# Two spectral mixings and two attentions on one core: first rows scaled and paired by TensorE, checks placed in the attention, the triangle added by TensorE in the last units, last rows folded by tile

## The chip, the core and the metric

The kernel runs on one core of a Trainium2 chip. The time is that of the device in microseconds, the median of several runs; the change is timed against the kernel before on the same chip. The engines are named as in the profile: PE (TensorE, matrix products; PEld are its weight loads), DVE (VectorE), ACT (ScalarE), POOL (GpSimd), SP (the engine that issues most transfers). A profile of one execution shows every instruction with its start and length and what it waited for.

## The reference

A sequence of 2048 rows of 512 numbers passes through four layers, each added to its input: `x = x + A(layernorm(x))`, then `x = x + B(layernorm(x))`, and both once more.

A is a Fourier mixing: the real part of a DFT over the sequence of a DFT over the hidden dimension, `y = Cr @ (x @ Wr) - Ci @ (x @ Wi)` with cosine and sine matrices that are inputs of the kernel.

B is an attention with 32 heads of 16 numbers over four segments of 512 rows. In a segment: causal softmax attention (`mask` adds -1e9 where the key is later than the query), and a read of a memory from the segments before it, `o = g * (phi(q) M) / (phi(q) z) + (1 - g) * softmax(q k^T / 4) v`. After each segment M and z grow by that segment's keys and values. Then `o @ wo`.

All is computed in float32 or in split forms that keep its precision.

## The kernel before, in words

**Folding.** The cosine and sine matrices are symmetric, so rows s, 1024 - s, 1024 + s and 2048 - s of the normalised input can be added and subtracted first, and the sequence DFT is made over an eighth of the rows. `place_folded` does this for a layer A. The rows lie in four groups A, B, C, D of two octants each, in two halves k = 0, 1; `quad(w, k)` is a tile of 128 partitions x 2 x 512. `normalise` computes mean and variance of each row (BATCH_NORM_STATS2, L376), the inverse root (a power on POOL, L381, and a Newton step on DVE), and scales in place (ACT L391, or DVE L389). `half` (L394) makes A-C (D01), A+C (S01), B-D (D32), B+D (S32); `fold_odd` (L400 to L406) mixes D01 and D32 into the tiles `re` and `im`; `fold_even` (L411 to L425) mixes S01 and S32. `contract(ps)` then makes the sequence DFT for one half ps of the output rows: steps `odd` and `even` for the kinds 0 (real) and 1 (imaginary) and the halves k. `odd` has 8 products of 256 columns (`u<-cf,hAB`), `even` 8 of 128 columns (`u<-cf,hS`) and some with a single row or a single column (`u<-rows`, `u<-cmid`). `drain` (L538 to L573) folds the sums back, `hidden(j)` makes the DFT over the hidden dimension and adds the input.

**Checks.** The folding is right only if the matrices given have the symmetry of a DFT. `place_checks` loads them in 68 units of 512 KB (`chk<-in_chk`, issued by SP, L686) and ACT compares each with one number per row (Abs with bias and running sum, L690, and a read of the sum). `verdict` adds all up and gives one bit; if it fails, a plain version follows. 34 units belong to each layer A: the first 20 from slot 6 to 24 of the layer, the others from slot 38 to 56, which is the start of the attention.

**Attention.** `place_attention` cuts a layer B into 32 units, (segment s, group of 8 heads g, half u of the group: 4 heads). For each: `stack` loads queries and keys (`stkq<-scrq`, `stkk<-scrk`, SP L858), which `proj` has stored as three bfloat16 parts; `natural_max` makes the scores row by row (`nat`) and takes each row's maximum on DVE (L887); `max_rows` turns the maxima (`mT`) and sends them into the query stack (`stkq<-mt`); `softmax_values` makes the scores again, transposed, with the maximum subtracted (`sT`), clamps the blocks on the diagonal (ACT Relu, L952), takes the exponential (ACT, L953, `pT`), zeroes the triangle above the diagonal (POOL select, L956), and multiplies by the values (`pv_bank`); `output` divides. `values`, `mem_read`, `mem_update`, `outproj` make the rest. In the last segment of attention 1, `finish` hands each output tile to `take`, which adds it straight into group D of the second fold (L352).

**Order.** Every function is a generator; `place(order, gen, slots)` says in which slots of a written timetable its steps are issued. Attention has 10 slots per unit. a1, b1, a2, b2 are the slots at which the four layers begin (b = a + 56, a2 = b1 + 340). This gives the program order. Products and transposes on PE keep it (`in_order`). On the other engines a planner orders by program order and priority, with its own estimate of when operands are there; `tc.high_priority(offset)` moves instructions ahead, `tc.issue_after(x)` puts an instruction behind x on the same engine. A tile's `tag` names a set of buffers: "wd" has 8, for probabilities `pT`, attention outputs `onat`, fold tiles and checks; "w" has 16, for the attention's weights; "bank" is 7 banks of PSUM and "pv" the eighth.

## Time and profile before

| | us |
|---|---|
| median of 3 runs | 1279.83 (1279.19 to 1283.01) |
| profiled execution | 1287.08 |
| its span, first to last instruction | 1284.9 |
| first product on PE | 23.67 |
| layer A 1 up to the first probabilities | 0 to 174 |
| attention 1 | 174 to 641 |
| layer A 2 and the attention's filling | 641 to 805 |
| attention 2 and the end | 805 to 1285 |

The profile divides the span into 40 slices of 32 us and gives for each engine the busy tenths. Windows give the busy us of each engine in a stretch, with the count of instructions, then the granted clock of PE (1.00 is full), the mean busy share of the 16 transfer engines and GB/s. A line of the timeline has start, length, engine, source line, operation, what is written `<-` what is read, shapes, how many instructions were merged, and in brackets how long the engine was idle before it and what ended that. Nearly all PE instructions carry L85, the helper that keeps their order, so they are told apart by the tiles.

### The profile page before, as it was taken

To read this page: it belongs to the slowest core of one execution; us is meant where nothing else is said; L and a number is where in the kernel's file an instruction comes from. 1 tells how busy PE (TensorE), PEld (TensorE's weight loads), DVE (VectorE), ACT (ScalarE), POOL (GpSimd) and SP (SyncE) were. 2 spreads that over 40 slices of the span, in tenths; PEclk is the share of its full clock that TensorE was granted. 3 is DMA by queue.
4 is the path that set the end of the run, shared out by engine and by line. 5 is a ranking of instruction groups with operands and counts; after the bars stand their busy time and mean duration, and the time that the engine had idled before them with its cause. 6 is when DMAs were issued, how large, how long until landed. Compare 5 with 4: busy or idle time off the path is not lost. (4 is left out here: it accounts for less than half of the span.)

```text
span 1284.9 us, 24191 instructions
## 1 busy us (share of the span) xinstructions
PE 1145.6 (89%) x7462; PEld 740.9 (58%) x7462; DVE 966.6 (75%) x3519; ACT 872.6 (68%) x1980; POOL 462.0 (36%) x826
## 2 busy tenths in 40 slices
PE   1999578999999999988779996989999999999987
PEld 1886344666566666554358864546665666666544
DVE  8777678778877777788485676867788777777872
ACT  2654677877677777777624546858876786778773
POOL 1021333534444444443300122524434443445431
PEclk9899889999999999999878998979998999999998
DMA  7787853433443344352426888524344334433411
GB/s 279 232 317 258 282 175 108 149 116 116 133 134 117 112 130 134 113 182 82 136 81 211 308 278 252 154 85 143 100 149 131 118 100 148 133 100 109 140 52 53
DMA packets 111094, 197.65 MB, mean 154 GB/s; under 512 B 13885, under 2 KB 63043, under 8 KB 110954
## 3 DMA queue, kind: packets, MB, share of 16 engines
q1 hardware_dynamic: 107690, 195.22, 47.6%
q8 instruction: 61, 1.00, 0.3%
q10 hardware_dynamic: 3264, 0.79, 0.3%
q14 instruction: 79, 0.65, 0.2%
HBM read 128.04 MB, written 67.14 MB: 152 GB/s over the span
## 5 line engine op out<-in xcount | busy, mean ns | idle before, releaser
L887 DVE CUSTOM_DVE_ANT_0 junk<-nat,mask 128x512 bf16<-128x512 f32 (+3 forms) x1024 | 500.6, 489 | 140.3 <-PE nat L85 107.4
L953 ACT ACTIVATE pT<-sT 128x512 f32<-128x512 f32 x640 | 370.6, 597 | 24.6 <-PE pv_bank L85 6.8
L956 POOL TENSOR_SCALAR_AFFINE_SELECT pT<-pT 128x256 f32<-128x256 f32 (+1 forms) x448 | 193.8, 446 | 469.9 <-ACT pT L953 429.9
L85 PE MATMUL nat<-stkk,stkq 96*128 96x512 bf16 (+3 forms) x1024 | 241.5, 307 | 46.6 <-DMA stkk<-scrk 19.6
L85 PE MATMUL sT<-stkq,stkk 99*128 99x256 bf16 (+3 forms) x1024 | 251.7, 311 | 20.7 <-DMA stkq<-mt 11.1
L952 ACT ACTIVATE sT<-sT 128x256 f32<-128x256 f32 (+1 forms) x640 | 208.8, 334 | 66.0 <-PE sT L85 58.2
L85 PEld LDWEIGHTS <-stkk 99*128 99x128 bf16 x1024 | 84.0, 100 | 149.4 <-issue 118.9
L85 PE MATMUL pv_bank<-pT,vt 128*17 128x512 f32 (+3 forms) x2048 | 157.0, 445 | 1.8 <-POOL pT L956 1.8
L85 PEld LDWEIGHTS <-stkq 96*128 96x128 bf16 x1024 | 94.3, 100 | 95.2 <-issue 59.9
L85 PE MATMUL pqk<-xT,wq 128*128 128x512 f32 x384 | 127.9, 446 | 4.6 <-ACT xT L97 2.6
L85 PE MATMUL po<-wo,oh 128*128 128x512 f32 x384 | 124.7, 444 | 3.8 <-DVE oh L99 3.0
L85 PE MATMUL pqk<-xT,wk 128*128 128x512 f32 x384 | 126.6, 442 | 0.0
L85 PE MATMUL pvv<-wv,xT 128*128 128x512 f32 x384 | 122.0, 432 | 2.8 <-DVE mx L887 2.8
L690 ACT ACTIVATE chk<-chk,reps 128x1024 f32<-128x1024 f32 (+1 forms) x80 | 81.3, 1017 | 60.4 <-DMA chk<-in_chk 60.1
L85 PEld LDWEIGHTS pv_bank<-pT,vt 128*17 128x17 f32 x2048 | 54.4, 99 | 87.8 <-issue 80.7
L85 PE MATMUL u<-cf,hAB 128*128 128x256 f32 x256 | 68.5, 429 | 34.2 <-DVE hAB L400 23.7
L1024 ACT ACTIVATE ot<-pv_bank 128x512 f32<-128x512 f32 x64 | 38.3, 598 | 70.6 <-PE pv_bank L85 70.6
L887 DVE DVE_READ_ACCUMULATOR2_ANT mx<- 128x1 f32 x1024 | 84.4, 82 | 0.2
L85 PEld LDWEIGHTS po<-wo,oh 128*128 128x128 f32 x384 | 70.3, 197 | 22.8 <-DVE oh L99 5.8
L827 POOL TENSOR_TENSOR parts<-rem,parts 128x512 bf16<-128x512 f32 x60 | 71.9, 1198 | 28.7 <-ACT parts L823 28.3
L85 PEld LDWEIGHTS u<-cf,hAB 128*128 128x128 f32 x256 | 54.7, 218 | 44.3 <-DVE hAB L400 23.7
L85 PEld LDWEIGHTS pqk<-xT,wq 128*128 128x128 f32 x384 | 70.2, 194 | 16.9 <-ACT xT L97 3.0
(200 smaller groups left out, 1673.5 us busy)
## 6 DMA issues: line engine op xcount, KB each, us to landing
chk<-in_chk SPq DMA_DIRECT2D x68, 512.0 KB
stkq<-scrq SPq DMA_DIRECT2D x64, 384.0 KB
stkk<-scrk SPq DMA_DIRECT2D x64, 384.0 KB
scrq<-parts SPq DMA_DIRECT2D x32, 384.0 KB
scrk<-parts SPq DMA_DIRECT2D x32, 384.0 KB
mid<-xrm SPq DMA_DIRECT2D x32, 256.0 KB
scrq<-parts SPq DMA_DIRECT2D x32, 256.0 KB
scrk<-parts SPq DMA_DIRECT2D x32, 256.0 KB
```

The lines of the kernel that those rows point to most:

```text
L85: return tc.keep_in_program_order(op(*args, **kwargs))
L690: A.activation(t[:, c : c + row], t[:, c : c + row], AF.Abs, bias=rep[:, col : col + 1], scale=scale, accum_out=acc[:, col : col + 1],)
L827: E.tensor_tensor(out=parts[:, 2], in0=rem, in1=parts[:, 1], op=ALU.subtract)
L887: V.tensor_tensor_reduce(junk[:, :n], src, mask[:, 512 - n :], 1.0, 3e38, ALU.add, ALU.min, dst,)
L952: A.activation(blocks, blocks, AF.Relu)
L953: A.activation(dst, ps, AF.Exp, scale=-SCALE)
L956: G.affine_select(blocks, blocks, pattern=[[0, n] for n in blocks.shape[1:-1]] + [[1, P]], compare_op=ALU.is_ge, fill=0.0, base=0, channel ...
L1024: A.activation(ot, pb, AF.Copy)
```

## The change

Four parts, and moves that go with them.

1. **First fold.** `open_folds` takes the place of `fold(0)`, `fold(1)` and `contract(0)` in the first layer. Rows are no longer scaled in place. ACT writes the inverse deviations as diagonal matrices (`diagonals`, plus and minus), and `level` lets PE form r_A*A - r_C*C or + by two products of 128x128 diagonals with 512 columns of float32. There are 16 such levels. The means enter as per-row constants: in ACT's copy out of PSUM (`away`) or in DVE's mix (`mixed`). The second half's statistics of three tiles are made on ACT (`on_a`). `warm` issues small products with the identity before the first levels. DVE, ACT and PE keep the written order here (`pinned`). The weights of the attention are loaded and split later (slot 14 on, before: 8 on), and constants that the opening doesn't need are made after it.
2. **Checks.** The 14 later units of each layer go to slots b + 85, b + 100, ... b + 280 of the attention. The first eight are loaded from slot -2 on into "w" buffers; ACT takes them behind the opening. The verdict goes to slot b2 + 305.
3. **Triangle.** In the last four units of each attention the clamp and the select fall away. A product of the mask (large where the key is later) with the identity is added to each diagonal block in PSUM, so that the exponential gives zero there. For the last three units `natural_max` and `max_rows` have earlier slots.
4. **Second fold.** `take` makes the statistics of each tile of group D as it comes, and `take_in(k, r)` scales and mixes it alone. A+C is made earlier with A-C. `odd` takes the later octant first there, and `contract(0)` has the order odd, odd, even, even for both halves.

The diff, cut to its core:

```diff
     def take(ps, xr, i):
         q, k = (6, i) if i < 2 else (7, 3 - i)
         dst = quad("D", k)[:, OCTANTS["D"].index(q)]
         xo = parts[i] = sb.tile([P, D], F32, name="xo", tag=("xn", "praw")[i % 2], bufs=2)
+        if "mv" not in row:
+            row["mv"] = sb.tile([P, LT, 2], F32, name="mvD", tag="mv", bufs=3)
+            row["own"] = sb.tile([P, LT, 2], F32, name="own", tag="norms", bufs=1)
+        mv, own = row["mv"], row["own"]
         with tc.high_priority(offset=URGENT):
             V.tensor_tensor(out=dst, in0=ps, in1=xr, op=ALU.add)
-            if i == 3:
-                V.tensor_copy(dst[0:1], parts[0][0:1])
-        if i == 3:
-            V.tensor_tensor(out=xo, in0=ps, in1=xr, op=ALU.add)
-        else:
+            bn(mv[:, i], dst)
+            if i != 1:
+                V.tensor_copy(own[0:1, i], mv[0:1, i])
+            for n, of in (*((n, of) for n, of in ENDS.items() if n == i), *(((2, 3),) if i == 3 else ())):
+                V.tensor_copy(mv[0:1, n], own[0:1, of])
             A.activation(xo, dst, AF.Copy)
-        for n, of, r, k in ((0, 2, 1, 0), (3, 3, 0, 1)):
-            if i == n:
-                A.activation(quad("D", k)[0:1, r], parts[of][0:1], AF.Copy)
+            for n, of, r, k in ((0, 2, 1, 0), (3, 0, 0, 0), (3, 3, 0, 1)):
+                if i == n:
+                    A.activation(quad("D", k)[0:1, r], parts[of][0:1], AF.Copy)
         return xo
     if late is not None:
         late.append(take)
+    def take_in(k, r):
+        i = {(6, 0): 0, (6, 1): 1, (7, 1): 2, (7, 0): 3}[OCTANTS["D"][r], k]
+        mv, x_ = row["mv"], quad("D", k)[:, r]
+        rr = sb.tile([P, 1], F32, name="rr", bufs=2)
+        ve, r_, t = (sb.tile([P, 1], F32, name=n, bufs=b) for n, b in (("ve", 3), ("r", 3), ("rt", 2)))
+        V.tensor_scalar_add(ve, mv[:, i, 1:2], EPS)
+        G.tensor_tensor(out=r_, in0=ve, in1=half_neg, op=ALU.pow)
+        V.scalar_tensor_tensor(t, r_, r_, ve, op0=ALU.mult, op1=ALU.mult)
+        V.tensor_scalar(t, t, -0.5, 1.5, op0=ALU.mult, op1=ALU.add)
+        V.tensor_mul(rr, r_, t)
+        V.tensor_scalar(x_, x_, mv[:, i, 0:1], rr, op0=ALU.subtract, op1=ALU.mult)
+        V.tensor_tensor(out=quad("D32", k)[:, r], in0=quad("B", k)[:, r], in1=x_, op=ALU.subtract)
+        fold_re(k, r)
+        V.tensor_tensor(out=quad("S32", k)[:, r], in0=quad("B", k)[:, r], in1=x_, op=ALU.add)
+        fold_im(k, r)
...
+        def on_a(mv, t, junk):
+            s_ = sb.tile([P, 2], F32, name="sums2", tag="st", bufs=2)
+            A.activation(junk, t, AF.Copy, accum_out=s_[:, 0:1])
+            A.activation(mv[:, 0:1], s_[:, 0:1], AF.Copy, scale=1.0 / D)
+            A.activation(s_[:, 1:2], s_[:, 0:1], AF.Copy, scale=-1.0 / D)
+            A.activation(junk, t, AF.Square, bias=s_[:, 1:2], accum_out=s_[:, 0:1])
+            A.activation(mv[:, 1:2], s_[:, 0:1], AF.Copy, scale=1.0 / D)
...
+            def diagonals(self):
+                k, g = self.k, self.g
+                for r in (1, 0):
+                    for n in (r, 2 + r):
+                        if n < 2:
+                            A.activation(diag[k][:, 4 * g + n], ident, AF.Copy, scale=self.rr[:, n : n + 1])
+                        else:
+                            A.activation(neg[:, 4 * k + 2 * g + r], ident, AF.Copy, scale=minus_rr[k][:, g, r : r + 1])
+                for n in (2, 3):
+                    A.activation(diag[k][:, 4 * g + n], ident, AF.Copy, scale=self.rr[:, n : n + 1])
...
+        def level(k, g, r, minus_):
+            spare[0] += 1
+            if spare[0] % 4:
+                ps = bank("fold")
+            else:
+                ps = psum.tile([P, 512], F32, name="fold", tag="pv", bufs=1)
+            a, c = ("AC", "BD")[g]
+            other = neg[:, 4 * k + 2 * g + r] if minus_ else diag[k][:, 4 * g + 2 + r]
+            T.matmul(ps, diag[k][:, 4 * g + r], quad(a, k)[:, r], start=True, stop=False)
+            T.matmul(ps, other, quad(c, k)[:, r], start=False, stop=True)
+            return ps
...
+        def mixed(out, d, const, e, op):
+            V.scalar_tensor_tensor(out, d, const, e, op0=ALU.add, op1=op)
...
+        def sums_of(k):
+            s_ = [(away("S01", k, r, level(k, 0, r, False)), level(k, 1, r, False)) for r in range(2)]
+            for r in range(2):
+                d, e = s_[r]
+                mixed(quad("C", k)[:, r], d, sums[k][:, 7, r : r + 1], e, ALU.add)
+                mixed(quad("D", k)[:, r], d, sums[k][:, 5, r : r + 1], e, ALU.subtract)
+        def away(name, k, r, ps, const=None):
+            t = quad(name, k)[:, r]
+            if const is None:
+                A.activation(t, ps, AF.Copy)
+            else:
+                A.activation(t, ps, AF.Identity, bias=const)
+            return t
...
+        def warm(gate, n):
+            ps = bank("warm")
+            T.matmul(ps[:, : gate.shape[1]], ident, gate, start=True, stop=True)
+            for _ in range(n):
+                T.matmul(ps[:, :P], ident, ident, start=True, stop=True)
...
+            ac, bd = Norm(0, 0), Norm(0, 1)
+            ac.stats(0, 1, 2, 3)
+            ac.root()
+            warm(ac.mv[:, 1], 16)
+            bd.stats(0, 1)
+            ac.newton()
+            ac.diagonals()
+            d_[0, 1] = away("S01", 0, 1, level(0, 0, 1, True))
+            d_[0, 0] = away("S01", 0, 0, level(0, 0, 0, True), sums[0][:, 0, 0:1])
+            warm(ac.mv[:, 1], 6)
+            bd.stats(2, 3)
+            bd.root()
+            bd.newton()
+            bd.diagonals()
+            both(0)
+            e_[0, 1] = level(0, 1, 1, True)
+            e_[0, 0] = away("S32", 0, 0, level(0, 1, 0, True), sums[0][:, 2, 0:1])
+            ac, bd = Norm(1, 0), Norm(1, 1)
+            bd.stats(0)
+            halves(0)
+            first_half(0)
+            odd(0, 0, 0)
+        yield
+        with pinned(on_v, on_s), urgent():
+            for i in range(3):
+                on_a(ac.mv[:, i], ac.tiles[i], quad("S01", 1)[:, 0])
+            bd.stats(1, 2, 3)
+            bd.root()
+            ac.stats(3)
+            bd.newton()
+            bd.diagonals()
+            ac.root()
+            sums_of(0)
+            ac.newton()
+            ac.diagonals()
+            both(1)
+            for r in (1, 0):
+                d_[1, r], e_[1, r] = away("S01", 1, r, level(1, 0, r, True)), level(1, 1, r, True)
+            thirds(0)
+            even(0, 0, 0)
+            halves(1)
+            first_half(1)
+            odd(0, 0, 1)
+        yield
+        with pinned(on_v, on_s), urgent():
+            sums_of(1)
+            odd(0, 1, 0)
+            odd(0, 1, 1)
+            even(0, 1, 0)
+            opened.extend((thirds(1), by_s[-1]))
+            even(0, 0, 1)
+        yield
+        drained.append(drain(0, 0)[0])
+        yield
+        even(0, 1, 1)
+        drained.extend(drain(0, 1))
...
-        for ab in range(2):
+        for n, ab in enumerate((0, 1) if late is None else (1, 0)):
...
-            steps = [(odd, 0, 0), (odd, 1, 0), (even, 0, 0), (even, 1, 0)]
-            steps += [(odd, 0, 1), (even, 0, 1), (odd, 1, 1), (even, 1, 1)]
+            steps = [(f, kind, k) for k in range(2) for f in (odd, even) for kind in range(2)]
...
-        t = pair("chk", "wd", 8, F32).rearrange("p a c -> p (a c)")
+        leads = k < LEADS
+        t = pair("chk", *(("w", 16) if leads else ("wd", 8)), F32).rearrange("p a c -> p (a c)")
...
-            A.activation(
-                t[:, c : c + row], t[:, c : c + row], AF.Abs,
-                bias=rep[:, col : col + 1], scale=scale, accum_out=acc[:, col : col + 1],
-            )
+            with after((opened, drained[:1], drained[1:2])[min(k // 2, 2)] if k < 20 else ()):
+                A.activation(
+                    t[:, c : c + row], t[:, c : c + row], AF.Abs,
+                    bias=rep[:, col : col + 1], scale=scale, accum_out=acc[:, col : col + 1],
+                )
...
+        added = turned and (s, g) >= (NSEG - 1, NG - 2)
...
-                    start=True,
-                    stop=True,
+                    start=not (added and diag),
+                    stop=not added,
+                    skip_group_check=added,
                 )
                 diag.append(off // P)
                 off += n
             blocks = ps.rearrange("p (b c) -> p b c", c=P)
             blocks = blocks[:, diag[0] : diag[-1] + 1 : max(1, diag[-1] - diag[0])]
-            A.activation(blocks, blocks, AF.Relu)
+            if added:
+                for n in range(len(diag)):
+                    T.matmul(
+                        blocks[:, n], mask[:, 384:], ident_b, start=False, stop=True, skip_group_check=True
+                    )
+            else:
+                A.activation(blocks, blocks, AF.Relu)
...
         def causal(blocks):
+            if added:
+                return
...
+        if turned and n >= NSEG * USEG - 3:
+            place(1.9, max_rows(*unit(n)), [t - 6])
+            place(1, natural_max(*unit(n)), [t - 16 + 2 * k // 3 for k in range(10)], [t - 9])
+        else:
+            place(1.9, max_rows(*unit(n)), [t - 4])
+            place(1, natural_max(*unit(n)), run_from(t - 16, 9), [t - 8, t - 7])
...
-        mids[0], mids[1], b1, ws, lambda k: a1 + 8 + 3 * k // 2 if k < 12 else b1 + 20 + 4 * (k - 12), lambda k: b1 + LB + 8 + k // 2,
+        mids[0], mids[1], b1, ws, lambda k: a1 + 14 + k if k < 12 else b1 + 20 + 4 * (k - 12), lambda k: b1 + LB + 8 + k // 2,
...
+    SPREAD = 85
     per = (len(folded.checks) + 1) // 2
     def check_at(k):
         early = 20
         n = k % per
-        t = (a1, a2)[k // per] + (6 + 18 * n // early if n < early else 38 + 18 * (n - early) // (per - early))
+        if k < 8:
+            return [a1 - 2 + k // 2, a1 + 6 + k // 3]
+        if n < early:
+            t = (a1, a2)[k // per] + 6 + 18 * n // early
+        else:
+            t = (b1, b2)[k // per] + SPREAD + 15 * (n - early)
         return [t, t + 3]
-    place(7, place_checks(check_at)(), [b2 + 40])
-    setup_at = 4
+    place(7, place_checks(check_at)(), [b2 + SPREAD + 220])
+    setup_at = [a1 - 12, a1 + 6]
```

More of the change, by code (lines that the diff above doesn't have):

```diff
@@ L150, in row_rsqrt, with after @@
         return mv, ve, r
-    first_row = []
+    first_row, opened, drained = [], [], []
+    @contextmanager
+    def after(what):
+        with ExitStack() as all_:
+            for i in what:
+                all_.enter_context(tc.issue_after(i.ins))
+            yield
     def behind_first(wanted):
@@ L345, in place_folded @@
         parts = {}
+        ENDS = {0: 2, 3: 0}
         def take(ps, xr, i):
```

216 lines of the change are left out of this document (149 added, 67 removed).

## The prediction

> **What bounds the kernel now.** I read the page first, then the waits of TensorE by stretch, then the order of time around its longest waits. The sums are made against the profiled execution: span 1284.9 us, 1287.1 us as a run, 7 us above the median of 1279.83. I carry differences over to the median unchanged. The page: busy time, then busy tenths in 40 slices of 32 us.
>
> ```profile
> PE 1145.6 (89%) x7462; PEld 740.9 (58%) x7462; DVE 966.6 (75%) x3519; ACT 872.6 (68%) x1980; POOL 462.0 (36%) x826
> ...
> PE   1999578999999999988779996989999999999987
> ...
> DMA  7787853433443344352426888524344334433411
> ```
>
> TensorE is the bound nearly everywhere. It is not in the first slice, in slice 5 (start of attention 1), around slices 18 to 21 (end of attention 1, fold 2) and at the end. The waits of TensorE in these places (total, times, longest, us):
>
> ```profile
> PE u L85 <- DVE hAB L400: 23.7, 1, 23.7
> ...
> PE nat L85 <- DMA stkk<-scrk: 14.0, 2, 12.7
> PE nat L85 <- ACT vt L779: 3.3, 1, 3.3
> ...
> PE u L85 <- issue: 8.2, 1, 8.2
> ...
> PE nat L85 <- DMA stkk<-scrk: 5.6, 1, 5.6
> PE mT L85 <- DVE mparts L910: 2.5, 2, 2.0
> PE sT L85 <- DMA stkq<-mt: 2.3, 1, 2.3
> ```
>
> The reader is to see four places: 23.7 us before the first product; 3.3 and 12.7 us about 150; 8.2 us about 660; 5.6, 2.0 and 2.3 us about 790. The change touches all four.
>
> **1. The opening.** In order of time:
>
> ```profile
> 8.38 1.02 POOL L381 TENSOR_TENSOR r<-ve,half_neg 128x4 f32<-128x4 f32 x1 [6.55 <-DVE ve L380]
> ...
> 11.66 1.52 ACT L391 ACTIVATE hAB<-hAB,nb,rr 128x512 f32<-128x512 f32 x2 [6.83 <-DVE nb L386]
> ...
> 23.67 3.78 PE L85 MATMUL u<-cf,hAB 128*128 128x256 f32 x8 [23.67 <-DVE hAB L400]
> 29.73 8.31 PE L85 MATMUL u<-cf,hAB 128*128 128x256 f32 x24 [2.28 <-DVE hAB L402]
> ...
> 54.88 3.62 PE L85 MATMUL u<-cf,hAB 128*128 128x256 f32 x16
> 58.34 1.95 PE L85 MATMUL u<-cf,hS 128*128 128x128 f32 x16
> 60.12 0.95 PE L85 MATMUL u<-cmid,hS 128*128 128x1 f32 x8
> 60.93 3.70 PE L85 MATMUL u<-cf,hAB 128*128 128x256 f32 x16
> ```
>
> A product is two records. From 54.88 to 58.34 eight products of 256 columns take 3.46 us, 0.43 each; from 58.34 to 60.12 eight of 128 columns take 0.22 each. So 512 columns cost 0.865 us, and contract(0) (32 products of 256 columns, 32 of 128, and 32 records of edge products, 0.12 us each by 60.12's row and more where the weights change, 5 us taken) costs 13.8 + 7.1 + 5 = 26 us. It took from 23.67 to 60.93, 37.3 us, because much of it ran at a low clock. After 29.73 TensorE no longer waits for VectorE here.
>
> The change takes from VectorE and ScalarE the scaling (L391, L389) and the eight half sums (L394) of the first fold, and gives TensorE 16 levels of two 512-column products: 16 x 2 x 0.865 = 27.7 us, more than its old wait of 23.7. They can't start before the first scales exist. These come by the old chain (statistics, the 1.02 us power, Newton steps), which gave ScalarE its first scaling at 11.66; I take 11. Then 11 + 1.3 (six warming products) + 27.7 + 26 = 66 us with no wait at all, 5 later than 60.93. Two waits come with the written order. The first odd step needs VectorE's last mix of half 0 (1.5 us). And the second half's diagonals stand behind three tiles' statistics on ScalarE and the sums of half 0 on VectorE, priced by the 0.76 us scaling above and this row:
>
> ```profile
> 22.87 0.75 DVE L400 SCALAR_TENSOR_TENSOR hAB<-hD,edge,hD 128x512 f32<-128x512 f32 x1
> ```
>
> Three tiles of two passes of 0.8 us with small steps behind each are, as an estimate, 6.6 us on ScalarE. The last of four half-0 levels ends about 31, two mixes of 0.75, Newton and two diagonals follow: TensorE waits 2.8 us. The clock (last but two of the columns):
>
> ```profile
> 42.00:44.00 2.00, 2.00 (x12) 2.00 (x12) 2.00 (x3) 0.63 (x1) 0.00 (x0) 0.60 0.90 296
> 44.00:46.00 2.00, 2.00 (x12) 1.97 (x11) 2.00 (x2) 0.63 (x1) 0.00 (x0) 0.55 0.76 299
> ```
>
> After the one-row edge products the granted clock was 0.60 and 0.55 for some 3.4 us with TensorE busy; the edge products stay, so I add 1.7 us for one such stretch. 66 + 1.5 + 2.8 + 1.7 = 72, **+11 us** (bounds +5, no wait; +16, two more such stretches and as much waiting again). What follows is TensorE's to the end of the stage, so all of it is passed on:
>
> ```profile
> 60.00:80.00 20.00, 20.00 (x99) 15.75 (x98) 12.70 (x35) 10.22 (x17) 1.46 (x5) 1.00 0.83 286
> 80.00:100.00 20.00, 17.93 (x110) 15.41 (x109) 16.05 (x36) 12.52 (x23) 5.01 (x9) 1.00 1.01 361
> ```
>
> The weight splits move behind the opening; VectorE has 4 to 7 us free in each of these stretches, so they cost nothing (twelve of 0.7 us, 8 us, if that cover were gone). The Trainium skill, TensorE: Matmul & The Clock Gate, Part 1, has the clock halve after an idle window and stay full under sustained products. The stretch above was busy and slow, so here the row decides; by the rule alone this term would be 9 instead of 11.
>
> **2. The checks leave the spectral stages.** Fourteen loads of 512 KB go from each stage's end into the attention; eight of the first stage's are also issued earlier, into buffers that the weights take later. Around the hole:
>
> ```profile
> 143.38 2.04 SPq L686 DMA_DIRECT2D chk<-in_chk  x4
> 148.32 0.89 SPq L686 DMA_DIRECT2D chk<-in_chk  x2
> ...
> 152.37 0.33 SPq L858 DMA_DIRECT2D stkk<-scrk  x1
> ...
> 164.22 0.59 PE L85 MATMUL nat<-stkk,stkq 96*128 96x512 bf16 x1 [12.68 <-DMA stkk<-scrk]
> ...
> 164.00:166.00 2.00, 1.78 (x7) 1.26 (x8) 1.16 (x3) 1.24 (x3) 0.00 (x0) 0.50 0.08 31
> ```
>
> Six checks (3 MB, about 10 us at the 286 to 361 GB/s of the two rows before) stand ahead of the stack load for which TensorE waits 12.7 us. The hole is 3.3 + 12.7 = 16 us, and the clock is at half behind it (0.50), 2 more. Some waiting stays while the units' chain of stores and loads fills; I leave 4. **-14 us** (bounds -18, -5). At 790 the holes are 5.6 + 2.3 + 2.0 and 2 of clock; 4 stay: **-8** (-12, -2).
>
> In the attention each check is on ScalarE's queue, ahead of the next softmax step, and takes one of eight buffers ("wd") that the probabilities use:
>
> ```profile
> L690 ACT ACTIVATE chk<-chk,reps x80: 489/1147/1186, 46.2 to 794.2; 128x1024 f32<-128x1024 f32 x64, 128x256 f32<-128x256 f32 x16
> L690 ACT ACTIVATION_READ_ACCUMULATOR chk<-chk,reps x80: 183/187/236, 47.3 to 794.6; 128x1 f32 x80
> ...
> 240.00:280.00 40.00, 40.00 (x287) 24.49 (x286) 31.03 (x125) 33.99 (x81) 20.12 (x31) 1.00 0.44 135
> ```
>
> 1.147 + 0.187 = 1.33 us each. ScalarE has 6 of 40 us free and the transfers run at 0.44; a check's load waits on SP's queue for a buffer, with stack loads behind it that are issued five slots early. The verdict moves with them, a few small instructions for which only the branch at the end waits. I take 0.15 us each for 28: **+4** (bounds 0; 37 if all of 1.33 is paid).
>
> **3. The last rows of fold 2, by tile.**
>
> ```profile
> 649.24 8.64 PE L85 MATMUL po<-wo,oh 128*128 128x512 f32 x36
> ...
> 652.32 0.69 DVE L352 TENSOR_TENSOR hD<-po,xr 128x512 f32<-128x512 f32 x1
> ...
> 655.12 0.69 DVE L352 TENSOR_TENSOR hD<-po,xr 128x512 f32<-128x512 f32 x1 [0.98 <-PE po L85]
> ...
> 657.96 0.68 DVE L352 TENSOR_TENSOR hD<-po,xr 128x512 f32<-128x512 f32 x1
> ...
> 666.10 9.29 PE L85 MATMUL u<-cf,hAB 128*128 128x256 f32 x32 [8.22 <-issue]
> ```
>
> TensorE ends the projection at 657.9 and waits until VectorE has statistics, scaling and halves of both tiles. Now statistics come with each tile, and tile i=0 (added at 652.3) is folded alone: its four odd products (1.7 us) can run at 658. Tile i=3 needs, after 655.1, an addition, statistics, copies, the power, scaling, difference and mix, with other tiles' additions between: about 663. That is 3 + 1.7, **-5 us** (bounds -9; 0, if VectorE's folding behind it sets the even steps anyway).
>
> **4. The triangle by TensorE** in the last four units of each attention. Per unit it removes ten clamps and seven selects, and adds 16 products of 128 columns; nearest for these is a weight load of such a product.
>
> ```profile
> L952 ACT ACTIVATE sT<-sT 128x256 f32<-128x256 f32 (+1 forms) x640 | 208.8, 334 | 66.0 <-PE sT L85 58.2
> L956 POOL TENSOR_SCALAR_AFFINE_SELECT pT<-pT 128x256 f32<-128x256 f32 (+1 forms) x448 | 193.8, 446 | 469.9 <-ACT pT L953 429.9
> ...
> L85 PEld LDWEIGHTS <-stkk 99*128 99x128 bf16 x1024 | 84.0, 100 | 149.4 <-issue 118.9
> ...
> 1220.00:1240.00 20.00, 17.36 (x135) 9.49 (x124) 18.00 (x78) 15.30 (x39) 6.64 (x17) 1.00 0.29 94
> ```
>
> ScalarE loses 3.3 us per unit and GpSimd 3.1, TensorE gains 1.6. With TensorE at 17.4 of 20 against 15.3 for ScalarE, the relief is mostly off the path, save the last unit of attention 1. **+1 us** (bounds: 8 x 1.6 = +13; -8, four us of chain in each attention). The earlier row maxima of three units go with it.
>
> Sum: 11 - 14 - 8 + 4 - 5 + 1 = **-11 us**: the span 1274, the median **1269 us**.
>
> **The rivals.** (a) The products of the opening hide in the old wait, since VectorE loses the eight half sums: term 1 is 0, **1258**. Against it: 27.7 is more than the 12 us between 11 and 23.67. (b) The holes are the filling of the units' chain, not the checks: 17 of the 22 us stay, **1286**. For it: SP issued the stack load only at 152.37; against it, twelve us from issue to use. (c) Slower: the checks in the attention. Each stops ScalarE, and TensorE behind it, for its whole 1.33 us: 37 instead of 4, **1302**. It decides from 0.67 us per check, where 28 checks eat the other -15 and 4 more. For it: TensorE's order is fixed; against it, ScalarE's free time. (d) The mask products are paid in full, +13 for +1: **1281**.
>
> **How the numbers follow.** No change means within 0.3%, 3.8 us, about what this measurement can tell. Forecast 0.46 (0.40 faster, 0.05 no change, 0.01 slower); (a) 0.20, all faster; (b) 0.11 (0.02, 0.04, 0.05); (c) 0.13 (0, 0.01, 0.12); (d) 0.10 (0.03, 0.06, 0.01). Together 0.65, 0.16, 0.19. The forecast's own range is 1258 to 1279; to leave out no more than two in ten it has to reach (a)'s faster half and (b): 1252 to 1290.
>
> **What would show it.** Term 1: the first contract(1) product (60.93 now) at 70 to 76; before 64 it is (a). Term 2: no wait of nat on a stack load over 4 us; if it stays with fewer transfers ahead of it, (b). Checks: TensorE's busy time in the attention's middle, 40.00 of 40 from 240 to 280 now; where it falls by over 0.6 us per check, it is (c). Term 3: the first odd product of fold 2 right behind the projection, the rest 3 to 5 us later. Term 4: in the last units a busy share of TensorE over 0.95 (17.36 of 20 now) speaks for (d). The forecast is wrong in kind if the opening gets shorter or the attention's middle gets longer.

## The result, and the profile after

The changed kernel takes 1287.86 us in the median (1281.26 to 1293.71), the kernel before 1280.12 beside it: a ratio of 1.0068, with a 95% interval of 1.0047 to 1.0090. It is slower by about 9 us, where I forecast 11 less. The profiled execution took 1286.16 us with a span of 1284.3.

The page of the changed kernel (busy time, then tenths in 40 slices, then the granted clock in tenths):

```profile
PE 1181.4 (92%) x7702; PEld 760.4 (59%) x7702; DVE 955.0 (74%) x3539; ACT 852.5 (66%) x1942; POOL 440.8 (34%) x772
...
PE   7898978999899999997879998989998999999987
...
PEclk9889989999999999999999998989999999999999
```

TensorE is busy 36 us longer in the same span. Slices 0 and 4 have filled (1 to 7 tenths, 5 to 9); the work that fills slice 0 was not there before. TensorE's waits (total, times, longest, us), by stretches up to 840 us:

```profile
PE fold L85 <- ACT hdiag L602: 3.8, 1, 3.8
PE u L85 <- DVE hre L85: 1.6, 1, 1.6
...
PE u L85 <- DVE ve L148: 2.5, 1, 2.5
...
PE mT L85 <- DVE mparts L1158: 2.1, 1, 2.1
...
PE u L85 <- issue: 3.5, 1, 3.5
```

The waits on stack loads of 12.7 and 5.6 us are gone, and the 8.2 us of the second fold are 3.5. In the second fold a second wait went as well, which the kernel before has behind the first:

```profile
PE u L85 <- DVE hS L418: 2.6, 1, 2.6
```

So the waits that the change aimed at did shrink. The opening in order of time:

```profile
11.89 1.02 PE L85 MATMUL fold<-hAB,hdiag 128*128 128x512 f32 x2
...
36.45 2.08 PE L85 MATMUL fold<-hAB,hdiag 128*128 128x512 f32 x2 [3.82 <-ACT hdiag L602]
38.32 1.91 PE L85 MATMUL fold<-hC,hminus 128*128 128x512 f32 x2
...
72.07 5.47 PE L85 MATMUL u<-cf,hS 128*128 128x128 f32 x32
...
78.19 3.70 PE L85 MATMUL u<-cf,hre 128*128 128x256 f32 x16
...
85.84 2.06 PE L85 MATMUL yi<-wf,vf 128*128 128x256 f32 x4
...
108.50 3.36 PE L85 MATMUL u<-cf,him 128*128 128x256 f32 x10 [2.52 <-DVE ve L148]
111.66 1.06 PE L85 MATMUL xnT<-ident,xn 128*128 128x128 f32 x4
```

The first contract(1) product comes at 78.19 (60.93 before; 70 to 76 forecast), and the first transposed row (xnT) at 111.66.

To see where time goes behind that, I use the 64 copies of a unit's outputs (ot) on ScalarE, whose first and last have these rows, in the changed kernel and in a second profiled execution of the kernel before (the first experiment):

```profile
L1282 ACT ACTIVATE ot<-pv_bank x64: 575/597/611, 188.0 to 1268.7; 128x512 f32<-128x512 f32 x64
```

```profile
L1097 ACT ACTIVATE ot<-pv_bank x64: 585/597/620, 166.4 to 1258.2; 128x512 f32<-128x512 f32 x64
```

The marks of the table are the first contract(1) product (c1), the first transposed row (xnT) of each spectral stage, and the start of these copies: "unit 4" is the fourth copy, units 33 to 64 are the second attention. Each column but the first gives the us from the mark before. Each row is one execution; those of e2 and e4 are the slowest of their kernels, that of e12 is the fastest of its own (1247.46 for a median of 1255.31).

| kernel | c1 at | to xnT | to unit 4 | 4 to 29 | 29 to 32 | to 2nd xnT | to unit 36 | 36 to 59 | 59 to 64 |
|---|---|---|---|---|---|---|---|---|---|
| before, first profile | 60.9 | 26.7 | 134.3 | 383.2 | 35.3 | 88.9 | 126.8 | 351.7 | 60.6 |
| before, again (e1) | 56.9 | 26.7 | 128.7 | 383.2 | 35.2 | 88.9 | 126.5 | 351.6 | 60.6 |
| changed | 78.2 | 33.5 | 120.1 | 391.7 | 28.1 | 79.7 | 117.6 | 357.1 | 62.8 |
| opening alone (e2) | 79.2 | 34.8 | 128.5 | 383.7 | 35.1 | 91.7 | 125.4 | 350.9 | 61.9 |
| checks alone (e3) | 59.2 | 26.6 | 117.1 | 391.2 | 35.8 | 92.0 | 118.9 | 358.6 | 63.5 |
| all but opening (e4) | 60.1 | 29.9 | 120.0 | 390.1 | 28.2 | 83.0 | 116.9 | 356.0 | 62.8 |
| rows and triangle (e5) | 56.7 | 28.2 | 128.5 | 382.1 | 28.1 | 79.8 | 130.4 | 351.8 | 60.2 |
| filled (e6) | 77.1 | 33.4 | 120.2 | 392.4 | 28.1 | 79.8 | 115.0 | 360.8 | 62.8 |
| splits on GpSimd (e7) | 78.8 | 30.1 | 123.1 | 392.1 | 28.1 | 80.5 | 117.9 | 356.5 | 63.2 |
| loads only (e8) | 60.5 | 26.6 | 121.1 | 381.6 | 28.1 | 77.9 | 115.9 | 351.2 | 60.8 |
| early loads (e9) | 59.9 | 26.6 | 120.5 | 391.7 | 28.1 | 80.5 | 117.9 | 358.1 | 61.6 |
| changed, early (e10) | 79.2 | 33.1 | 118.4 | 390.6 | 28.2 | 80.7 | 115.2 | 358.4 | 64.6 |
| other buffers (e11) | 56.4 | 26.7 | 119.9 | 388.1 | 28.5 | 79.2 | 118.3 | 357.6 | 61.1 |
| work only (e12) | 56.7 | 26.6 | 116.7 | 387.6 | 28.1 | 79.3 | 115.2 | 357.1 | 60.8 |

Columns of kernels that share a part agree within 1 to 3 us in most places and within 6 at worst, and that makes the stages readable. Some of the spread is the granted clock: to xnT, kernels with the old opening take 26.7 us without half clock, e5 28.2 with one stretch of 3.4 us at half clock and e4 29.9 with two. From e1 to the changed kernel the columns give +21.3, +6.8, -8.6, +8.5, -7.1, -9.2, -8.9, +5.5 and +2.2: together +10.5, against +8.7 by the ratio of the medians.

### The profile page after: what moved, and what is told of

The parts are those of the page before. It is cut to its first block, busy times and chain, and to the rows that moved or that the text cites. A ratio compares the mean times of both kernels' runs of the same rounds, so it can differ in the third digit from the quotient of the medians.

```text
span 1284.3 us, 24540 instructions
## 1 busy us (share of the span) xinstructions
PE 1181.4 (92%) x7702; PEld 760.4 (59%) x7702; DVE 955.0 (74%) x3539; ACT 852.5 (66%) x1942; POOL 440.8 (34%) x772
## 4 chain that ended last, share of the span: by engine, by line
PE 61%; DVE 16%; ACT 8%; DMA 6%; issue 6%; POOL 2%; ACTq 0%; SPq 0%; DVEq 0%; POOLq 0%
PE pv_bank L85 9%; PE pqk L85 8%; DVE junk L1135 8%; PE sT L85 8%; PE u L85 7%; PE nat L85 7%; PE pvv L85 5%; PE po L85 5%; DMA chk<-in_chk 4%; ACT pT L1209 2%; PE pm L85 2%; PE fold L85 2%; PE pM L85 2%; ACT sT L1208 1%; PE yr L85 1%
## 5 line engine op out<-in xcount | busy, mean ns | idle before, releaser
L1214 POOL TENSOR_SCALAR_AFFINE_SELECT pT<-pT 128x512 f32<-128x512 f32 x392 | 170.6, 448 | 385.1 <-ACT pT L1209 346.3
L85 PE MATMUL nat<-stkk,stkq 96*128 96x512 bf16 (+3 forms) x1024 | 237.7, 304 | 18.7 <-DVE mx L1135 16.4
L1208 ACT ACTIVATE sT<-sT 128x256 f32<-128x256 f32 (+1 forms) x560 | 182.0, 335 | 55.1 <-PE sT L85 51.3
L85 PE MATMUL pv_bank<-pT,vt 128*17 128x512 f32 (+3 forms) x2048 | 154.0, 440 | 0.0
L85 PEld LDWEIGHTS <-stkq 96*128 96x128 bf16 x1024 | 93.0, 99 | 65.7 <-issue 28.2
L85 PE MATMUL pqk<-xT,wk 128*128 128x512 f32 x384 | 126.5, 442 | 1.3 <-ACT pT L1209 0.6
L1135 DVE DVE_READ_ACCUMULATOR2_ANT mx<- 128x1 f32 x1024 | 84.5, 83 | 0.0
L1319 POOL TENSOR_TENSOR onat<-onat,otmp 128x128 f32<-128x128 f32 x96 | 47.7, 504 | 102.6 <-DVE otmp L1318 99.5
L1075 POOL TENSOR_TENSOR parts<-rem,parts 128x512 bf16<-128x512 f32 x60 | 71.6, 1194 | 29.5 <-ACT parts L1071 26.7
L85 PEld LDWEIGHTS pvv<-wv,xT 128*128 128x128 f32 x384 | 68.8, 193 | 16.2 <-DVE mx L1135 4.6
L85 PEld LDWEIGHTS pqk<-xT,wk 128*128 128x128 f32 x384 | 68.9, 195 | 13.7 <-ACT pT L1209 0.8
```

The costliest lines, as they stand in the source:

```text
L85: return tc.keep_in_program_order(op(*args, **kwargs))
L1075: E.tensor_tensor(out=parts[:, 2], in0=rem, in1=parts[:, 1], op=ALU.subtract)
L1135: V.tensor_tensor_reduce(junk[:, :n], src, mask[:, 512 - n :], 1.0, 3e38, ALU.add, ALU.min, dst,)
L1208: A.activation(blocks, blocks, AF.Relu)
L1214: G.affine_select(blocks, blocks, pattern=[[0, n] for n in blocks.shape[1:-1]] + [[1, P]], compare_op=ALU.is_ge, fill=0.0, base=0, channel ...
L1319: G.tensor_tensor(out=dst, in0=dst, in1=tmp, op=ALU.add)
```

## The experiments

Times are medians; ratios are to the kernel before on the same chip, with 95% intervals.

**e1: the kernel before, profiled again.** No edit.

> The kernel before, unchanged, profiled a second time. The first profiled execution took 1287.1 us, 7 above its median, and my sum was made against it. Theory 1 (the excess is in the holes near 150 and 790, whose length varies from execution to execution): this profile is nearer to 1280, and its first copy of a unit's outputs (ot, 176.6 us in the first profile) or the same in the second attention comes 4 to 8 us earlier, with the opening the same within 1 us. Theory 2 (the excess is the granted clock, spread over the span): the holes are as long as before (16 us near 150), and the mean granted clock is over 0.952 by 0.005 or more with all stages a little shorter.

The profiled execution has a span of 1273.4 us, 11.5 less than the first one (1275.54 median, ratio 0.9979, 0.9947 to 1.0012). Of the difference 9.6 us lie ahead of unit 4: 4.0 in c1, 5.6 in the stretch with the hole. From there to the last copy the two agree within 0.3 us in every column; 1.4 lie behind it. The hole here (waits up to 205 us):

```profile
PE nat L85 <- ACT chk L753: 10.1, 1, 10.1
...
PE nat L85 <- ACT vt L842: 1.9, 1, 1.9
```

It was 12.7 and 3.3 in the execution that I summed against. c1 differs by two stretches of half clock (42 to 46 and 49 to 53 us in the first profile) which this execution doesn't have. Theory 1 holds in part: the excess sits in one hole and in the opening's clock, not at 790, and the mean clock (0.958 against 0.952) follows from that.

**e2: the opening alone.** Checks and triangle as before, and the old functions take, fold and odd for the last rows.

```diff
-    t = (b1, b2)[k // per] + SPREAD + 15 * (n - early)
+    t = (a1, a2)[k // per] + 38 + 18 * (n - early) // (per - early)
-    added = turned and (s, g) >= (NSEG - 1, NG - 2)
+    added = False
...
```

> The kernel before with the new opening alone (its checks leave the spectral stages as before, old fold of the last rows, no triangle on TensorE). Theory 1 (the opening costs what the changed kernel's trace shows): the first contract(1) product at 77 to 79 us and the time 12 to 24 us over the kernel before, since the hole near 150 is not shortened. Theory 2 (the hole behind FNet 1 is fixed by the transfers of the checks, which don't depend on the opening, so a later TensorE falls into it): contract(1) at 77 to 79 too, but the hole shrinks by 8 or more, and the time is 0 to 8 us over the kernel before.

1304.47 us, ratio 1.0215 (1.0185 to 1.0245): 27 us slower. Theory 1. Its marks:

```profile
79.19 3.70 PE L85 MATMUL u<-cf,hre 128*128 128x256 f32 x16
...
113.98 0.88 PE L85 MATMUL xnT<-ident,xn 128*128 128x128 f32 x4
```

c1 is 22.3 later than in e1 and the stage behind it 8.1 longer. The stretch with the hole is as long as in e1 (128.5 against 128.7): the hole absorbs none of it.

**e3: the checks alone.** The first edit of e2 the other way round, on the kernel before.

> The kernel before with 28 checks moved into the attentions and nothing else. Theory 1 (as the changed kernel's trace reads: holes -12 and -8, checks in the attention +10 instead of my +4): -6 to -14 us. Theory 2 (the holes are the filling of the units' chain): they stay at over 10 us near 150, and the time is +2 to +14. Theory 3 (my forecast, checks nearly free in the attention): -16 to -20.

1285.71 us, ratio 1.0058 (1.0028 to 1.0088): slower. The stages show what was exchanged. The two stretches with holes get shorter by 11.6 and 7.6, the two attentions longer by 8.0 and 7.0, and 59 to 64 by 2.9. So none of the three came out: holes as in theories 1 and 3, but the checks cost nearly all of it again. The stages don't show the whole loss. These columns come to -1.3 us; what makes this execution 4.7 us longer than e1 lies in c1, 29 to 32 and to the second xnT, where the edit does nothing, and the execution profiled (1279.93 us) was faster than the median.

**e4: all but the opening.** The changed kernel with the old opening (old fold, order of contract(0), weight loads, setup and early checks).

> The changed kernel with the old opening: checks moved, last rows folded by tile, triangle on TensorE. Theory 1 (the opening alone makes the change slower, parts add up): 1260 to 1270 us. Theory 2 (the parts hide in one another: without the opening's later TensorE the hole near 150 comes back, or the attentions pay for the checks): 1274 to 1284.

1260.12 us, ratio 0.9865 (0.9840 to 0.9889). Theory 1. The opening costs 27 us alone and 26 on top of the rest (1.0068 - 0.9865 = 0.0203 of 1280).

**e5: rows and triangle.** e4 with the checks back in the spectral stages (the edit of e2).

> The kernel before with the last rows folded by tile and the triangle on TensorE, and nothing else (old opening, all checks in the spectral stages). Theory 1 (parts add up as the stages of the runs so far read: the rows gain about 9 in fold 2, the triangle about 8, nearly all at the end of the first attention, the moved checks cost about 5 over the whole): 1255 to 1262 us on a scale where the kernel before is 1277, so below the run that has the moved checks too (1260). Theory 2 (the moved checks and these parts need each other: without the checks gone from the stages the rows' gain is lost behind the hole near 790): 1266 to 1274.

1263.92 us, ratio 0.9905 (0.9868 to 0.9943), between the two theories. Both parts show in their stages: 9.1 less to the second xnT, 7.1 less from unit 29 to 32. But the stretch behind grows by 3.9 (130.4 against 126.5), in these waits:

```profile
PE nat L85 <- DVE sums L765: 7.8, 1, 7.8
PE sT L85 <- DMA stkq<-mt: 4.3, 1, 4.3
PE u L85 <- issue: 3.3, 1, 3.3
```

With the checks still in the stage, TensorE reaches the hole earlier and waits longer there: nat 7.8 us and sT 4.3, where the first profile had 5.6 and 2.3. With the checks moved (e4) that stretch is 116.9. So the move of the checks, a loss by itself, is worth 13.5 there once the rows are folded early. Over the whole time e4 and e5 are hardly told apart: their intervals overlap.

Why the fourth part is worth 7 and not 0: the waits of TensorE from 594 to 634 us in the kernel before (e1), and in e5, where the maxima of these units come earlier:

```profile
PE sT L85 <- DMA stkq<-mt: 5.8, 2, 4.5
PE pv_bank L85 <- POOL pT L1029: 1.9, 1, 1.9
```

```profile
PE sT L85 <- DMA stkq<-mt: 0.8, 1, 0.8
```

The added products, again in e5, by order of time:

```profile
606.60 0.39 PE L85 MATMUL sT<-stkq,stkk 99*128 99x384 bf16 x2
606.83 0.28 PE L85 MATMUL sT<-ident_b,mask 128*128 128x128 bf16 x2
606.95 0.38 PE L85 MATMUL sT<-stkq,stkk 99*128 99x384 bf16 x2
```

From 606.83 to 606.95, a pair takes 0.12 us: 1 us per unit. Of the waits that are gone, 5.0 us are those for the row maxima and 1.9 that for the select. So the earlier slots of the maxima, a move that goes with the triangle, are the larger part by this reading; no run separates the two.

**e6: the wait of the opening filled.** The changed kernel with 15 products ahead of the second half's first level:

```diff
+    for _ in range(fill):
+        T.matmul(ps[:, :P], ident, ident, start=True, stop=True)
     T.matmul(ps, diag[k][:, 4 * g + r], quad(a, k)[:, r], start=True, stop=False)
```

> The changed kernel with 15 warming products (128 columns) written into the first bank of the second half's levels, where TensorE waits 3.8 us for its diagonals at 32.6 to 36.45. Theory 1 (the half clock behind the wait is set by TensorE's idleness): six products behind it take 0.86 each instead of 1.6 to 0.9, the first contract(1) product comes 2.2 to 3.2 us earlier. Theory 2 (the half clock is set by something else, such as the load before): the products behind it are as slow as before, contract(1) within 0.7 us or later by the fill.

```profile
32.38 3.62 PE L85 MATMUL fold<-ident 128*128 128x128 f32 x30
36.24 1.13 PE L85 MATMUL fold<-hAB,hdiag 128*128 128x512 f32 x2 [0.24 <-ACT hdiag L604]
37.21 1.02 PE L85 MATMUL fold<-hC,hminus 128*128 128x512 f32 x2
...
47.33 5.38 PE L85 MATMUL u<-cf,hre 128*128 128x256 f32 x16
```

The products behind the wait run at full speed, and the even step starts at 43.21 instead of 45.92: 2.7 earlier, as theory 1 has it. But the eight odd products behind the one-row products then take 5.38 us, for 3.72 in the changed kernel: half clock again. c1 is 1.06 earlier, 77.13, and not the 2.2 to 3.2 of theory 1; the ratio 1.0048 (1.0020 to 1.0076) is not to be told from 1.0068.

**e7: weight splits on GpSimd.**

```diff
-    split(w[:, 0], w[:, 1], raw)
+    split(w[:, 0], w[:, 1], raw, lo_engine=V if name == "wo" else G)
```

> The changed kernel with the subtraction of the weight splits (q, k, v) on GpSimd instead of VectorE, which has twelve of 0.7 us in the stage behind the opening. Theory 1 (the stage from the first second-layer product, yi, to the first transposed row, xnT, is 25.8 us instead of 19.0 because VectorE got these splits): 21 to 23 us there, the wait of 2.5 us on ve gone, and the time 3 to 5 us below the changed kernel. Theory 2 (it is the half clock behind the one-row products, 84 to 90 us): the stage stays at 25 to 27 and the time within 2 us of the changed kernel.

1285.91 us, ratio 1.0060 (1.0033 to 1.0088). The stage to xnT is 3.4 shorter, the wait on ve is gone, and the next stretch is 3.0 longer:

```profile
PE mT L85 <- DVE mparts L1158: 6.0, 2, 3.5
```

Theory 1 is right about the stage, theory 2 about the time: the splits do slow the stage, but TensorE then waits for VectorE in the next one. In the changed kernel it waits there 2.1 us for these maxima and 2.3 for another step of VectorE's; 1.6 of the 3.0 us are in this wait, the rest is not placed.

**e8: loads only.** e4, with ScalarE's part of the 28 moved checks left out.

```diff
-    with nullcontext():
+    if k % ((len(folded.checks) + 1) // 2) < 20:
         A.activation(
```

> The run with all but the opening, from which ScalarE's work of the 28 checks in the attentions is left out; their loads stay. From the fourth to the 29th unit that run lost 7 us in the first attention, and 3 to 4 in the second up to the 57th. Theory 1 (a check costs by ScalarE's time, 1.33 us, ahead of the softmax): the loss is 0 to 1.5 in each attention, the time 8 to 12 us below that run (1248 to 1252 where the kernel before is 1277). Theory 2 (it costs by its buffer or its place on SP's queue): the loss stays at 5 or more, the time within 3 us of that run.

1241.83 us, ratio 0.9723 (0.9684 to 0.9762): 18 us below e4, more than the 8 to 12 of theory 1. Units 4 to 29 and 36 to 59 take 381.6 and 351.2, no more than in the kernel before; these columns hold 13.3 us of the profiled difference, and 8.4 lie in the two up to xnT, where e4 has more half clock. SP's queue waits for a buffer at these loads as it does in e4 (14.8 and 15.7 us in the first attention). So neither the buffers nor SP's queue cost anything by themselves: it is what ScalarE does with the checks. One of them, ScalarE's order of time in e4 with TensorE's next product:

```profile
492.35 0.60 ACT L1027 ACTIVATE pT<-sT 128x512 f32<-128x512 f32 x1
494.76 1.15 ACT L756 ACTIVATE chk<-chk,reps 128x1024 f32<-128x1024 f32 x1 [1.82 <-DMA chk<-in_chk]
495.81 0.19 ACT L756 ACTIVATION_READ_ACCUMULATOR chk<-chk,reps 128x1 f32 x1
495.91 0.57 ACT L1100 ACTIVATE ot<-pv_bank 128x512 f32<-128x512 f32 x1
...
496.54 0.66 PE L85 MATMUL on<-ident,ot 128*128 128x128 f32 x4 [1.25 <-ACT ot L1100]
```

The same place in e8:

```profile
487.33 0.60 ACT L1027 ACTIVATE pT<-sT 128x512 f32<-128x512 f32 x1
488.42 0.60 ACT L1100 ACTIVATE ot<-pv_bank 128x512 f32<-128x512 f32 x1 [0.49 <-PE pv_bank L85]
```

The copy of the outputs starts 3.56 us behind the last probability in e4, 1.09 in e8. In between ScalarE first waits 1.82 us for the check's data and then works on it for 1.33, ahead of the copy for which TensorE waits. Which of the two costs more is what the last four runs ask.

**e9 and e10: loads eight slots ahead**, on e4 and on the changed kernel.

```diff
     t = (b1, b2)[k // per] + SPREAD + 15 * (n - early)
+    return [t - 5, t + 3]
```

> The run with all but the opening, in which the load of each of the 28 moved checks is issued eight slots ahead of its work instead of three. In that run ScalarE sat idle 4.0 us in the first attention and 6.5 in the second until a check's load landed, with the softmax and TensorE behind it. Theory 1 (of the 18 us that the checks' presence on ScalarE costs, these late loads are most): the idle time falls below 1.5 in each attention and the time is 8 to 12 us below that run (0.978 to 0.981 of the kernel before). Theory 2 (the 1.33 us of work ahead of the softmax is most): 0 to 4 us below it (0.984 to 0.987). Theory 3 (earlier loads hold buffers and SP's queue that the probabilities and stacks need): slower than that run.

> The changed kernel with the same earlier loads. Theory 1 (late loads): 8 to 12 us below the changed kernel, 0.997 to 1.000 of the kernel before, so the opening then stands alone for the rest of the loss. Theory 2 (the work itself): 1.003 to 1.007.

1259.15 us, ratio 0.9860 (0.9826 to 0.9894), and 1286.21 us, ratio 1.0069 (1.0039 to 1.0098): no difference. But the edit hadn't done what it was for. In e9 ScalarE's idle time ahead of these checks in the first attention grew (4.0 us in two waits in e4):

```profile
  DMA chk<-in_chk: 7.1, 6
```

**e11: other buffers.** e9, with the moved checks in the two buffers of the set "craw".

```diff
-    t = pair("chk", *(("w", 16) if leads else ("wd", 8)), F32).rearrange("p a c -> p (a c)")
+    t = pair("chk", *(("w", 16) if leads else ("craw", 2) if k % ((len(folded.checks) + 1) // 2) >= 20 else ("wd", 8)), F32).rearrange("p a c -> p (a c)")
```

> The run with loads eight slots ahead (0.986), in which the moved checks are read into two buffers that the attention doesn't use otherwise, instead of eight shared with the probabilities. In that run the earlier place alone had not brought the data earlier: ScalarE still sat idle 7.1 and 5.4 us for them, and SP's queue waited 22 and 24 us at these loads until the products with the values (pv_bank) had freed a buffer. Theory 1 (late data is most of the 18 us): the idle time falls below 1 in each attention, and the time is 8 to 12 us lower (0.976 to 0.980). Theory 2 (the work of 1.33 us itself): the idle time falls as much, but the time by 4 at most (0.983 to 0.987).

1252.41 us, ratio 0.9790 (0.9749 to 0.9830). The buffers are not the checks' own, as the expectation has it: the attention reads the third probability tile of each unit (`pT2`) into this set, and SP's queue waits longer for a buffer at these loads than before. Its waits in the first attention, in e9 and in e11:

```profile
SPq L751 <- PE pv_bank L85: 22.1, 6, 5.8
```

```profile
SPq L751 <- PE pv_bank L85: 34.4, 7, 6.3
```

The data came in time all the same. ScalarE's idle time fell to

```profile
  DMA chk<-in_chk: 1.0, 1
```

in the first attention and 0.7 in the second. The time is theory 1's. Units 4 to 29 and 36 to 59 together take 745.7, which is only 4.1 less than in e9 and about what e4 takes (746.1). The rest of the profiled gain lies outside the attentions, where the edit does nothing: 3.5 us are in c1, before which e9 has three stretches of half clock and e11 one.

**e12: work only.** e11 without 26 of the 28 loads; ScalarE works on data that are there.

> The run with own buffers, from which 26 of the 28 loads of the moved checks are left out: ScalarE does the same 28 pieces of work (1.33 us each for the wide ones) on data that are there already, and their sums are not used. It is the counterpart of the run with loads only, which took 0.972 of the kernel before; own buffers took 0.979, shared ones 0.986. By stage, the units 4 to 29 of the first attention and 36 to 59 of the second took 382 + 351 us without ScalarE's checks and 388 + 358 to 392 + 358 with them. Theory 1 (the data's lateness is most of what is left): 382 to 384 + 351 to 353, time 0.970 to 0.974. Theory 2 (the work itself, ahead of the softmax): 387 to 391 + 356 to 358 as with loads, time 0.977 to 0.983.

1255.31 us, ratio 0.9840 (0.9798 to 0.9881), just above the range of theory 2. The two columns, 387.6 and 357.1, are those of theory 2 as well: 12 us over e8's 732.8. But the run doesn't answer its question. Without loads the planner drew the 14 checks of an attention together (264 to 346 us in the first, for 267 to 581 in e11), so they stand in other places. A finer cut of the same copies shows it, in us for both attentions together. "Net" is without what the half clock takes, counting a stretch of 3.4 us as 1.7:

| | units 4 to 25 and 36 to 53 | net | units 25 to 29 and 53 to 59 | net |
|---|---|---|---|---|
| before, again (e1) | 592.6 | 584.0 | 142.3 | 140.6 |
| loads only (e8) | 590.3 | 585.1 | 142.5 | 140.8 |
| changed | 599.9 | 591.3 | 148.9 | 147.2 |
| all but opening (e4) | 597.8 | 591.0 | 148.3 | 144.9 |
| early loads (e9) | 603.0 | 594.5 | 146.8 | 143.4 |
| other buffers (e11) | 592.1 | 588.7 | 153.6 | 146.8 |
| work only (e12) | 603.3 | 596.5 | 141.4 | 141.4 |

In e11 the first units hold 21 checks of 1.33 us, spread out and nearly all with their data there. They cost nothing against e1, and 4.7 us net: 0 to 0.2 us each. In e4 and e9, where ScalarE waits for data, the same units take 6 and 11 us more than in e11, 2 and 6 net. The loss of e12 lies where its checks stand close together: units 8 to 13 and 40 to 45 take 91.5 and 91.7 us, for 84.8 and 84.6 in e8 and 84.5 and 84.7 in e11; behind them nothing is lost. So for a check that stands alone the work costs 0.2 us at most, and with late data it costs 0.1 to 0.5 more. That this is ScalarE's waiting, and not the buffer that a check holds until it is done, is likely by e4's rows, but no run separates the two.

More than half of what e11 loses is in the other units, in a few places. The largest is the unit behind copy 53, 5.8 us longer than in e8 with 3.4 us more lost to half clock:

```profile
1088.24 1.15 ACT L756 ACTIVATE chk<-chk,reps 128x1024 f32<-128x1024 f32 x1 [0.67 <-DMA chk<-in_chk]
...
1089.39 0.25 ACT L991 ACTIVATE mt<-mT 48x128 bf16<-48x128 bf16 x1
...
1090.88 0.73 ACTq L992 DMA_DIRECT2D stkq<-mt  x1
```

This check came ahead of the copy of the row maxima (mt), which are then sent to the query stack, and TensorE waits 3.6 us for them. The rest is mostly in the last units of the first attention, where four narrow checks of 0.7 us, the form of 4 of the 28 units, stand between the steps of the second fold; there the cause is not separated.

Kernels with ScalarE's moved checks take 745 to 750 in the two columns of the first table (753 in e6), those without 733 to 735. So a moved check costs 0.4 to 0.6 us in the mean, but it is not a price per check: most cost little, and a few cost several us. The median of e11 is lower than those of e9 and e12 by 3 to 7 us. Part of that goes with the granted clock, whose median over the executions is 0.9735 in e11 and 0.9705 in the other two; within each kernel the time falls as the clock rises (e11: 1258.7 us at 0.970, 1246.3 at 0.978). e11 is the fastest complete kernel here, 25 us below the kernel before and 35 below the changed one; how much of that is the buffers stays open, by the stages about 4 us.

## Why the prediction was wrong, step by step

**The base.** "I carry differences over to the median unchanged" failed for an execution 7 us above its median, whose excess lay in the very places that the change removes. The first hole's -14 is exact against the profile that I used (134.3 to 120.1) and -8.6 against an execution near the median. A sum has to ask where an execution's excess lies.

From -11 to +9 there are 20 us. The opening was 16 too low, the checks in the attention 12 and the holes 4.5; the rows and the triangle came out better than forecast, by 4 and 8.5.

**1. The opening: +11 forecast, +27 alone.** The mechanism was right, the size not. c1 forecast at 72, measured 78.2. By the terms: start 11.9 for 11 (+0.9); waits of 1.6, 3.8 and 0.3 for 4.3 (+1.4); half clock behind the 3.8 wait, where three products, one level and a half, take 5.2 us (36.45 to 41.63) for 2.6 (+2.6), which I hadn't counted; levels, contract(0) and warming products +1.3. The half clock behind the edge products was as forecast (72.07: 5.47 for 3.6). These make +6.2. Then the base: executions of the old opening start contract(1) at 56 to 61, mean 58.6, not at 60.93 (+2.3). Behind c1, to xnT it took 33.5 for 26.7, +6.8. Of this 3.5 are waits for VectorE (2.5 of it in the row at 108.50), and they are the weight splits, which I had costed at nothing: on GpSimd (e7) the stage is 3.4 shorter, though the time is not. Most of the rest is two half-clock stretches, at 86 to 89 and from 110 us on, which are not shown to be the opening's, since e4 has two in this stage as well. 11 + 6.2 + 2.3 + 6.8 = 26. I had named 8 us for the case that the cover was gone, and left it out of the bound. So the terms that failed are the half clock behind the opening's own wait and the splits, both put at nothing, and the start of the old opening, taken from one late execution. Neither of the first two gives the time back alone: with the wait filled (e6) or the splits moved (e7) it is the same within the intervals.

**2. The checks.** The holes: -14 and -8 forecast, -8.6 and -8.9 measured, and the waits on stack loads disappeared as I had said. The checks in the attention: +4 forecast, +16 in the changed kernel (8.5 + 5.5 + 2.2). The step that failed is "I take 0.15 us each", reasoned from "ScalarE has 6 of 40 us free". As the price of the work it is about right for a check that stands alone and has its data: e11 shows 0 to 0.2 us. What it put at nothing is where a check stands in ScalarE's order. In the changed kernel ScalarE sits idle 4.8 and 6.1 us in the two attentions until a check's load lands, although I had written that the load waits for a buffer, and e4's rows show the copy of the outputs, and TensorE, behind that wait. And a few checks stand ahead of a copy on which TensorE's next products hang, as in e11 at 1088. My sign for it was badly chosen too: TensorE's busy time from 240 to 280 is 40.00 of 40 in the changed kernel as well, where the first moved check runs only at 295.

**3. The last rows: -5 forecast, -9.2.** TensorE still waits 3.5 us of the 8.2 (my -5, nearly), but the wait of 2.6 on hS behind it went too. The rest goes with the clock: TensorE is busy at half clock for 9.2 us of this stage in the changed kernel and for 14.6 in e1, a difference of 2.7 us; a new wait of 1.0 on hAB takes some of it back. It was my bound.

**4. The triangle: +1 forecast, -7.5**, 7.1 of it at the end of the first attention. I priced relief per unit and looked at busy shares of the last units of the second attention, where it is worth 0.4 (60.2 for 60.6). In the first one the chain of row maxima held TensorE for 5.8 us, 4.5 of them at once, and the select for 1.9; I had "four us of chain" as a bound only, and didn't read the waits from 594 to 634.

**The rivals.** (a) fell: products start 11.8 us earlier in the old wait, but c1 comes 17 us later than in the profile before and 21 later than in e1. (b) fell: with the loads gone the holes are gone. (c) named the right loser, as e3 shows by itself, but not the mechanism: not each check stops TensorE for its whole work, the mean is 0.4 to 0.6 us, below the 0.67 from which (c) decides, and it comes in the main from late data and from a few bad places. (d) fell. None had the opening at +27. The time lies in the range, near its upper end, on the side that I gave 0.19.

## What to carry to other kernels

Work given to the engine that bounds the kernel costs its full time wherever the wait that it is to fill is shorter, and it can pay the half clock behind a new wait, as here behind 3.8 us; count it against a typical start, not against one profile. A piece of work put on an engine with free time is priced by whether its data are there when its turn comes, by the instruction that stands behind it in that engine's order and by who waits for that one; its own length and the share of free time say little. Before summing gains, take a second profile: the stage in which two executions of one kernel differ is where differences can't be carried over.

## What the runs showed of the hardware that I had not expected

In the spectral stages the granted clock falls to one half in stretches of 3.4 us or twice that also while the profile shows TensorE busy all the time, behind runs of products with one row or one column. In e4 the same products as in every kernel, by 1 us (the last but two of the columns is the clock):

```profile
67.00:68.00 1.00, 1.00 (x6) 0.76 (x6) 0.00 (x0) 0.12 (x2) 0.00 (x0) 1.00 1.07 438
68.00:69.00 1.00, 1.00 (x4) 0.81 (x4) 0.00 (x0) 0.84 (x1) 0.00 (x0) 0.73 1.03 422
69.00:70.00 1.00, 1.00 (x3) 0.34 (x1) 0.71 (x2) 0.89 (x3) 0.00 (x0) 0.50 0.78 299
...
75.00:76.00 1.00, 1.00 (x3) 0.66 (x4) 0.64 (x3) 0.00 (x0) 0.21 (x1) 0.86 1.16 236
```

It is half from 68.5 to 75.3, 6.8 us; in e1, at the same products (64 to 72 us), it stays 1.00. The Trainium skill (TensorE: Matmul & The Clock Gate, Part 1) gives the gate a free-running window of about 3.4 us; the lengths agree, and a window that runs free would explain why the same products are caught in one execution and not in the next, which no run here tests. What it says of idle windows doesn't cover these, as far as the profile shows: TensorE was busy. But the ends of products are modelled in the profile, so short gaps inside such a run can't be excluded. Behind a wait, less idle time than one such window was enough: in the changed kernel the last product ahead of the 3.8 us wait ended at 32.6, and the clock fell about 2 us later:

```profile
34.00:36.00 2.00, 0.00 (x0) 0.00 (x0) 1.90 (x7) 0.00 (x0) 0.00 (x0) 0.67 1.04 351
36.00:38.00 2.00, 1.54 (x2) 0.84 (x3) 1.93 (x9) 1.86 (x6) 0.00 (x0) 0.50 0.43 175
```

In e6 the fill took this stretch away, and the next run of one-row products was caught in its place.
